# Attention beside a state-space convolution: the skip term goes into the first tap, and the recurrence coefficients are computed per group of chunks

## The chip, the cores and the metric

One core of a Trainium2 chip (trn2) runs the whole program. Its engines are named as in the profile: PE (matmul; PEld are its weight loads), DVE (elementwise work), ACT (activation functions), POOL and SP, which issue transfers. The metric is the device time of one execution in microseconds (us), lower is better.

## The reference

Two independent halves are computed and laid side by side in the output. Half A is a convolution of 2048 steps whose kernel comes from a diagonal complex recurrence; half B is attention with 32 query heads that share one key and one value head.

```python
# A: L = 2048, D = 576 channels, N = 128 states per channel
dt = exp(log_dt)[:, None];  logdA = dt * (A_re + 1j * A_im);  dB = dt * (B_re + 1j * B_im)
P = exp(logdA[:, :, None] * arange(L))                  # powers of the recurrence
K = einsum("dn,dnl,dn->dl", C_re + 1j * C_im, P, dB).real   # one kernel of 2048 taps per channel
y = irfft(rfft(u padded to 2L) * rfft(K padded to 2L))[:L] + u * Dskip
# B: S = 2048, H = 32 heads of 18
q = (x @ wq) by heads;  k = x @ wk;  v = x @ wv
out = softmax(q @ k.T * 18**-0.5) @ v, heads put together, @ wo
```

`u * Dskip` is the skip term. A convolution adds `u[t] * K[0]` to `y[t]`, so `Dskip` can as well be added to `K[0]`, the first tap.

## The kernel before

**Attention.** `main` walks over 1024 tiles of scores (four blocks of 512 queries, 16 pairs of heads, 16 blocks of 128 keys), three tiles to a round. For each tile PE computes the scores `s` (`scores`, L516), ACT takes the exponential into a tile `P` (L527), and PE multiplies by the values into `ops` (L817), a product of four matmuls per two tiles. Query projections `q` (L408) and output projections `op` are work of PE that is put between the rounds. What is left of the last output projection when the last exponential is done is computed in `finish` (`fin`).

**Convolution.** The 576 channels are cut into twelve chunks of 48. `front(k)` makes the kernel of chunk k: `factors` and `tables` (DVE) build tables of powers, `kgen` (PE) multiplies them, and the result goes from `ksb` through DRAM (`kd`) into `kt`, 128 partitions with the first tap in partition 0. `back(k)` convolves: `transform` takes u to its spectrum `us` (matmuls `hu`, `lu`), then `kt` to `ks` (matmuls `hk`, `lk`), DVE multiplies the two (`pt`, `acc`, `sv`, `w`), and the inverse (`iy`) gives the output in `ut`, whose tile is called `u` in the profile. `back(k)` and `front(k + 1)` run beside each other, and both beside the attention. Powers are computed for groups of chunks at once (`BURSTS`: chunk 0, chunks 1 to 4, 5 to 8, 9 to 11), at the group's first chunk.

**What sets the order.** All instructions of PE, DVE and ACT stand in an order that a planner in the kernel makes while the program is built. It keeps its own clocks for PE, DVE and ACT (`Clock`), and the streams of work are Python generators: `yield "p", ready` means that PE work comes next, `yield "v", ready` DVE work; a DVE step is let through when PE's clock has reached `ready` and DVE's clock is at most `ahead` (0.7 to 1.7) past PE's. `lag` compares the convolution's DVE work with `step * RATE`. Engines work through their instructions strictly in this order. All transforms, projections and `kgen` share a single PSUM tile, `f` (`bank`): the next user waits until DVE has copied the previous result out. SP's queue is in program order too.

**Places that the change touches.** `coefficients(k)` (L1046), called for each chunk in `factors` (L1185), computes the products of B, C and dt into `w` by seven DVE instructions on tiles `raw` that `load` (L1012) fetches chunk by chunk. The skip term: `load_u` (L1033) fetches `dsk`, the chunk's `Dskip` broadcast over all partitions, and at the end of `back` DVE computes `ut * dsk` (L1395), to which the results of `iy` are added out of PSUM (L1408):

```python
tt(ut, ut, dsk.unsqueeze(1).broadcast_to([P, 4, NE]), op=ALU.mult)
for hf in range(2):
    ...
    tt(ut[:, sl, :], ut[:, sl, :], ps, op=ALU.add)
```

All DVE instructions that go through the helper `Vector` carry its line in the profile (L119 for two inputs, L123 for copies, L127 for a scalar).

Of the kernel before, what the change touches and what calls it, by code (L numbers as in the profile page):

```python
# [9 lines left out]
F32 = mybir.dt.float32  # L10
# [3 lines left out]
ALU = mybir.AluOpType  # L14
# [3 lines left out]
P = 128  # L18
# [44 lines left out]
ND = 48  # L63
NCK = D // ND
NSB = 2
TB = ND // 4 // NSB
NE = 4 * ND
NF = 28
NB = 11
BURSTS = ((0, 1), (1, 5), (5, 9), (9, 12))  # L70
# [906 lines left out]
class Conv:  # L977
# [31 lines left out]
        pool = lambda n, b: ctx.enter_context(self.tc.tile_pool(name=n, bufs=b))  # L1009
        self.p1 = pool("s_1", 1)  # L1010

    def load(self, k):  # L1012

        if k >= NCK:
            return
        raw = self.p0.tile([P, 4, ND], F32, tag="raw", name=f"raw{k}")
        self.nc.sync.dma_start(raw, self.a["prm"][k])
        self.raw[k] = raw

    def load_burst(self, g):  # L1020

# [11 lines left out]
    def load_u(self, k):  # L1033
        if k >= NCK:
            return
        nc = self.nc
        ut = self.p0.tile([P, 4, NE], F32, tag="u", name=f"u{k}")
        if k < 2:
            nc.vector.memset(ut[0:1, 0, 0:1], 0.0)
        dsk = self.p0.tile([P, NE], F32, tag="dsk", name=f"dsk{k}")  # L1040
        nc.sync.dma_start(ut, self.a["u"][k])
        nc.sync.dma_start(dsk, self.a["dsk"][k].partition_broadcast(P))
        self.ut[k] = ut, dsk
        self.ut_ready[k % 2] = self.k.t + 10.0

    def coefficients(self, k):  # L1046


        V, p1 = self.V, self.pf
        tt = V.tensor_tensor  # L1050
        mu, ad, sb = ALU.mult, ALU.add, ALU.subtract
        raw = self.raw.pop(k)
        w = p1.tile([P, 3, ND], F32, tag="w", name=f"w{k}")
        dt = self.dt[:, (k - self.k0) * ND:(k - self.k0 + 1) * ND]
        tt(raw[:, 0:2, :], raw[:, 0:2, :], dt.unsqueeze(1).broadcast_to([P, 2, ND]), op=mu)
        br, bi, cr, ci = (raw[:, j, :] for j in range(4))
        tt(w[:, 0, :], cr, br, op=mu)
        tt(w[:, 2, :], ci, bi, op=mu)
        tt(w[:, 0, :], w[:, 0, :], w[:, 2, :], op=sb)
        tt(w[:, 1, :], cr, bi, op=mu)  # L1060
        tt(w[:, 2, :], ci, br, op=mu)
        tt(w[:, 1, :], w[:, 1, :], w[:, 2, :], op=ad)
        return w

    def powers(self, g):


        nc, V, p1, K = self.nc, self.V, self.pf, self.k
        tt = V.tensor_tensor
        mu, ad, sb = ALU.mult, ALU.add, ALU.subtract  # L1070
        self.k0, k1 = BURSTS[g]
        nch = k1 - self.k0
        n = nch * ND
        dt, ab = self.next_burst
        self.dt = dt
        shp = [P, n, NB]
        flat = lambda t: t.rearrange("p (n c) -> p n c", c=NB)
        if g == 0:
            both = p1.tile([P, 2, ND * NB], F32, tag="sum", name="pw0")
            r, f = flat(both[:, 0, :]), flat(both[:, 1, :])  # L1080
        else:
            both = p1.tile([P, 2, ND // NSB, 96], F32, tag="tab", name=f"stage{g}").rearrange("p j n c -> p (j n c)")
            r, f = (flat(both[:, j * n * NB:(j + 1) * n * NB]) for j in range(2))
        m = flat(p1.tile([P, 2 * ND * NF], F32, tag="fr", name=f"m{g}")[:, :n * NB])
        ch = lambda t: t.unsqueeze(2).broadcast_to([P, t.shape[1], NB])
        row = lambda j, c: self.pos[:, j, :].unsqueeze(1).broadcast_to([P, c, NB])
        parts = [slice(i * n // (2 if g else 1), (i + 1) * n // (2 if g else 1)) for i in range(2 if g else 1)]
        nc.scalar.activation(dt, dt, AF.Exp)
        yield "v", K.act(0.35) + 0.2, False
        tt(ab, ab, dt.unsqueeze(1).broadcast_to([P, 2, n]), op=mu)  # L1090
        av, bv = ab[:, 0, :], ab[:, 1, :]
        V.tensor_scalar(bv, bv, 1.0 / (2 * math.pi), None, op0=mu)
        yield "v", 0.0, False
        if g > 0:
            for c in parts:
                tt(m[:, c, :], ch(av[:, c]), row(1, c.stop - c.start), op=mu)
                yield "v", 0.0, False
        for c in parts:
            tt(f[:, c, :], ch(bv[:, c]), row(0, c.stop - c.start), op=mu)
            yield "v", 0.0, False  # L1100
        V.tensor_scalar(r, f, MAGIC, -MAGIC, op0=ad, op1=ad)
        yield "v", 0.0, False
        for c in parts:
            tt(f[:, c, :], f[:, c, :], r[:, c, :], op=sb)
            yield "v", 0.0, False
        V.tensor_scalar(r.bitcast(I32), f.bitcast(I32), 0x7FFFFFFF, None, op0=ALU.bitwise_and)
        if g == 0:
            nc.scalar.activation(f, f, AF.Sin, scale=TWO_PI)
            yield "v", 0.0, False
            tt(m, ch(av), row(1, n), op=mu)  # L1110
        else:
            nc.scalar.activation(m, m, AF.Exp)
            K.act(0.1 + 0.833e-3 * n * NB)
        yield "v", 0.0, False
        if g == 0:
            for k in (1, 2):
                self.load(k)
            yield "v", K.v + 0.3, False
        self.burst = g > 0
        yield "b", K.v + 0.3, False  # L1120
        nc.scalar.activation(r, r, AF.Sin, scale=-TWO_PI, bias=self.hp)
        if g > 0:
            nc.scalar.activation(f, f, AF.Sin, scale=TWO_PI)
        else:
            nc.scalar.activation(m, m, AF.Exp)
        yield "v", K.act(3.3 + 1.67e-3 * n * NB) + 0.3, False
        for t in (r, f):
            for c in parts:
                tt(t[:, c, :], t[:, c, :], m[:, c, :], op=mu)
                yield "v", 0.0, False  # L1130
        if nch > 1:
            self.kept = self.dr.tile([P, nch - 1, 2, ND * NB], F32, tag="pw", name=f"pw{g}")
            for j, t in enumerate((r, f)):
                nc.sync.dma_start(self.kept[:, :, j, :], t[:, ND:, :].rearrange("p (k n) c -> p k (n c)", n=ND))
            self.stored = K.t + 9.0
        self.pw = r[:, 0:ND, :], f[:, 0:ND, :]
# [8 lines left out]
    def factors(self, k):  # L1145
# [3 lines left out]
        tt = V.tensor_tensor  # L1149
# [32 lines left out]
        x3 = lambda t: t[:, :, 8:11].unsqueeze(3).broadcast_to([P, ND, 3, 3])  # L1182
        product(x3(pr), x3(pi), r8[:, :, :, 1:4], f8[:, :, :, 1:4], r8[:, :, :, 5:8], f8[:, :, :, 5:8], t1, t2)
        yield "v", 0.0, False
        w = self.coefficients(k)  # L1185
        if k > 0:
            self.load(k + 2)
        if k + 1 == BURSTS[g][1]:
            self.load_burst(g + 1)
        yield "v", 0.0, False  # L1190
# [69 lines left out]
    def front(self, k):  # L1260

        nc = self.nc
        yield from self.factors(k)
        ksb = self.pf.tile([P, 4, NSB, 16, TB], F32, tag="ksb", name=f"ksb{k}")
        yield "v", self.stored, False
        for s in range(NSB):
            yield from self.tables(k, s)
            if s == NSB - 1 and all(k + 1 not in (k0, k1) for k0, k1 in BURSTS):
                self.restore(k + 1)
            yield from self.kgen(k, s, ksb)  # L1270
        while self.kt is not None:
            yield "w", 0.0, False
        kt = self.p1.tile([P, 4, NSB, 16, TB], F32, tag="kt", name=f"kt{k}")
        kd = self.dr.tile([P, 4, NSB * 16 * TB], F32, tag="kd", name=f"kd{k}")
        nc.sync.dma_start(kd, ksb.rearrange("p h s c d -> p h (s c d)"))
        for h in range(4):
            nc.sync.dma_start(kt[32 * h:32 * h + 32].rearrange("p g s c d -> p g (s c d)"), kd[:, h].rearrange("(g p) x -> p g x", p=32))
        self.kt, self.kt_ready = kt, self.k.t + 9.0
# [51 lines left out]
    def back(self, k, kt):  # L1330
# [6 lines left out]
        yield "v", 0.0, False  # L1337
        tt(us[:, 0:4, :], us[:, 4:8, :], us[:, 8:12, :], op=ALU.add)
        ks = p1.tile([P, 12, NE], F32, tag="ks", name=f"ks{k}")
        yield from self.transform(lambda r: kt[:, :, :, 4 * r:4 * r + 4, :].rearrange("p g s b d -> p (g s) (b d)"), ks[:, 4:12, :], f"k{k}", self.kt_ready)  # L1340
        self.kt = None
        k2, kd, ka = ks[:, 0:4, :], ks[:, 4:8, :], ks[:, 8:12, :]
# [48 lines left out]
        tt(w[:, 1:8:6, :], bd[:, 0:2, :], bd[:, 2:4, :], op=ALU.subtract)  # L1391
        tt(w[:, 3:6:2, :], bd[:, 0:2, :], bd[:, 2:4, :], op=ALU.add)
        ready = K.v + 0.3
        yield "v", 0.0, False
        tt(ut, ut, dsk.unsqueeze(1).broadcast_to([P, 4, NE]), op=ALU.mult)  # L1395
        for hf in range(2):
            yield "p", max(ready, K.fill), False
            ps = self.bank(2 * NE, f"iy{k}{hf}").rearrange("p (r n) -> p r n", r=2)
# [6 lines left out]
                if r % 2 == 0:  # L1405
                    yield "p", 0.0, True
            self.evacuate()
            tt(ut[:, sl, :], ut[:, sl, :], ps, op=ALU.add)  # L1408
            self.evacuated()
        nc.sync.dma_start(self.a["outa"][k], ut)  # L1410
        self.load_u(k + 2)
# [83 lines left out]
def layout(inputs):  # L1495

    g = {k: np.asarray(v) for k, v in inputs.items()}
    a = {}
# [30 lines left out]
    a["u"] = np.ascontiguousarray(g["A_u"][0].reshape(4, P, 4, NCK, NSB, 4, TB).transpose(3, 1, 2, 5, 4, 0, 6).reshape(NCK, P, 4, NE))  # L1529
    a["pa"] = np.ascontiguousarray(np.stack([g["A_" + k].T for k in ("A_re", "A_im")], 1))  # L1530
    prm = np.stack([g["A_" + k].T for k in ("B_re", "B_im", "C_re", "C_im")])
    a["prm"] = np.ascontiguousarray(prm.reshape(4, P, NCK, ND).transpose(2, 1, 0, 3))
    a["ldt"] = np.ascontiguousarray(g["A_log_dt"])
    dsk = g["A_Dskip"].reshape(NCK, NSB, 4, 1, TB).transpose(0, 2, 1, 3, 4)
    a["dsk"] = np.ascontiguousarray(np.broadcast_to(dsk, (NCK, 4, NSB, 4, TB)).reshape(NCK, NE))
    i = np.arange(P)[:, None].astype(np.int64)
    f = np.arange(P)[None, :].astype(np.int64)
    th = [2 * np.pi * (((4 * f + 1) * (4 * i + r)) % 2048) / 2048.0 for r in range(4)]
# [30 lines left out]
```

## Time and profile before

| | |
|---|---|
| time, median of 3 runs | 1157.36 us (1155.91 to 1157.46) |
| the profiled execution's own time | 1158.43 us |
| its span in the profile | 1156.7 us |
| granted PE clock, mean | 0.993 |
| PE busy | 1083.0 us (94%) |
| ACT busy | 998.6 us (86%) |
| DVE busy | 995.8 us (86%) |
| moved by DMA | 83.37 MB, mean 72 GB/s |

Times of instructions are in us from the span's start. In the groups of instructions a row reads: line, engine, operation, result and input tiles with shapes, count, then busy time in us, mean ns of one, and idle time of the engine just before them with the instruction that ended it. An fp32 matmul stands in the profile as two records, so x16 in a row of `hk` are eight instructions. Busy time counts overlapping instructions of an engine once.

### The profile page before, as it was taken

How to read it: one execution, taken by the hardware profiler on the slowest of the kernel's cores; microseconds unless marked ns; L12 is line 12 of the kernel's file. 1: busy time of each engine (PE TensorE's matmuls, PEld its weight loads, DVE VectorE, ACT ScalarE, POOL GpSimd, SP SyncE). 2: the span in 40 equal slices, each digit the busy share in tenths (PEclk: the TensorE clock that was granted, in tenths of full speed). 3: DMA queues.
4: the chain of work that ended last, by engine and by line, in shares of the span. 5: the costliest groups of instructions: out<-in, count | busy, mean ns of one | idle time of the engine just before them, and what ended most of it. 6: DMA issues, size and time to landing. Idle time of an engine off the chain costs nothing.

```text
span 1156.7 us, 33067 instructions
## 1 busy us (share of the span) xinstructions
PE 1083.0 (94%) x13886; PEld 393.1 (34%) x13886; DVE 995.8 (86%) x1739; ACT 998.6 (86%) x1052; POOL 141.5 (12%) x257
## 2 busy tenths in 40 slices
PE   6999899999999999899999999989999999999997
PEld 1333333324334333323333333334323333323323
DVE  3788996998998998898899798997898899799683
ACT  3889998888888998998898989887999989899992
POOL 5321322022022000001022000001050000000000
PEclk9999999999999999999999999999999999999999
DMA  7412331114123102112222302102122200311101
GB/s 226 140 46 73 125 119 50 52 42 143 36 74 101 40 28 93 58 40 87 82 85 77 104 21 74 48 29 91 46 84 77 87 30 29 105 48 47 58 29 58
DMA packets 58751, 83.37 MB, mean 72 GB/s; under 512 B 14467, under 2 KB 34679, under 8 KB 58085
## 3 DMA queue, kind: packets, MB, share of 16 engines
q1 hardware_dynamic: 47173, 73.39, 19.2%
q0 software_dynamic: 10848, 7.37, 2.5%
q8 instruction: 111, 1.82, 0.6%
q10 hardware_dynamic: 576, 0.43, 0.2%
q14 instruction: 43, 0.35, 0.1%
HBM read 46.59 MB, written 33.85 MB: 70 GB/s over the span
## 4 chain that ended last, share of the span: by engine, by line
PE 59%; DVE 21%; ACT 12%; issue 6%; DMA 1%; POOL 1%; ACTq 0%; DVEq 0%; POOLq 0%
PE ops L817 24%; PE s L516 15%; ACT P L527 11%; PE op L193 5%; PE q L408 4%; DVE tab L119 4%; PE iy L193 3%; DVE ks L119 3%; PE kg L1253 3%; DVE acc L119 2%; DVE t L119 2%; PE hu L193 1%; PE hk L193 1%; DVE fr L119 1%; PE fin L193 1%
## 5 line engine op out<-in xcount | busy, mean ns | idle before, releaser
L527 ACT ACTIVATE P<-s 128x1024 f32<-128x1024 f32 x992 | 934.6, 1033 | 113.8 <-PE s L516 111.5
L817 PE MATMUL ops<-P,v_sb 128*32 128x512 f32 x4096 | 510.4, 599 | 8.1 <-DVE o L123 7.8
L516 PE MATMUL s<-aug,kaug 55*128 55x512 f16 x2048 | 308.2, 381 | 37.3 <-ACT P L527 33.4
L516 PEld LDWEIGHTS <-kaug 55*128 55x128 f16 x2048 | 91.0, 94 | 372.3 <-issue 326.7
L817 PEld LDWEIGHTS ops<-P,v_sb 128*32 128x32 f32 x4096 | 117.0, 110 | 164.8 <-issue 128.3
L458 POOL DMA_DIRECT2D qd<-qh x116 | 65.6, 572 | 309.6 <-DVE qh L127 307.0
L408 PE MATMUL q<-x,wq_sb 128*32 128x256 f32 x1360 | 83.7, 382 | 0.1
L193 PE MATMUL op<-wo_sb,oT 126*32 126x288 f32 (+1 forms) x1080 | 78.5, 416 | 2.6 <-DVE ob L123 1.4
L119 DVE TENSOR_TENSOR tab<-tab,tt 128x576 f32<-128x576 f32 (+1 forms) x72 | 59.1, 821 | 1.4
L119 DVE TENSOR_TENSOR tab<-tab 128x576 f32<-128x576 f32 (+1 forms) x72 | 58.8, 817 | 0.0
L119 DVE TENSOR_TENSOR tab<-fr,dif 128x576 f32<-128x576 f32 (+1 forms) x72 | 58.8, 817 | 0.0
L119 DVE TENSOR_TENSOR tt<-fr,sum 128x576 f32<-128x576 f32 (+1 forms) x72 | 58.8, 817 | 0.0
L119 DVE TENSOR_TENSOR tab<-sum,fr 128x576 f32<-128x576 f32 (+1 forms) x72 | 58.8, 817 | 0.0
L123 DVE COPY ksb<-kg 128x192 f32<-128x192 f32 x48 | 17.5, 364 | 46.9 <-PE kg L1253 46.6
L408 PEld LDWEIGHTS q<-x,wq_sb 128*32 128x32 f32 x1360 | 39.4, 109 | 38.5 <-issue 13.9
L119 DVE TENSOR_TENSOR acc<-acc,pt 128x1728 f32<-128x1728 f32 (+2 forms) x36 | 48.7, 1352 | 0.1
L119 DVE TENSOR_TENSOR pt<-us,ks 128x1728 f32<-128x1728 f32 (+2 forms) x36 | 48.4, 1351 | 0.1
L1162 POOL MEMSET fr<- 128x192 f32 x24 | 11.9, 580 | 294.0 <-DVE tt L119 192.2
L193 PEld LDWEIGHTS op<-wo_sb,oT 126*32 126x32 f32 (+1 forms) x1080 | 30.6, 110 | 44.2 <-issue 18.3
L525 ACT ACTIVATE P<-s,bias 128x1024 f32<-128x1024 f32 x32 | 32.8, 1123 | 12.9 <-PE s L516 12.7
L1253 PEld LDWEIGHTS kg<-tab 128*32 128x32 f32 x2304 | 35.7, 110 | 22.7 <-DVE ksb L123 7.6
L1253 PE MATMUL kg<-tab 128*32 128x64 f32 x2304 | 41.8, 220 | 1.2 <-DVE tab L119 0.8
(160 smaller groups left out, 1022.4 us busy)
## 6 DMA issues: line engine op xcount, KB each, us to landing
od<-o SPq DMA_DIRECT2D x31, 256.0 KB
aug<-qd SPq DMA_DIRECT2D x124, 55.0 KB
u<-u SPq DMA_DIRECT2D x12, 384.0 KB
kd<-ksb SPq DMA_DIRECT2D x12, 384.0 KB
kt<-kd SPq DMA_DIRECT2D x48, 96.0 KB
outa<-u SPq DMA_DIRECT2D x12, 384.0 KB
pw<-pw SPq DMA_DIRECT2D x8, 528.0 KB
oT<-od SPq DMA_DIRECT2D x16, 252.0 KB
```

The lines of the kernel that those rows point to most:

```text
L119: return self.v.tensor_tensor(out, *a, **k)
L123: return self.v.tensor_copy(out, *a, **k)
L193: nc.tensor.matmul(ps[j:e], w[:, j:e], x, start=start, stop=stop, tile_position=(0, j))
L408: nc.tensor.matmul(ps[o, 256 * f:256 * f + 256], w[:, k, i], xt[:, k, x], start=(k == 0), stop=(k == 4), tile_position=(0, 32 * j))
L458: q.dma_start(qd[h:h + n, row + d:row + d + nd, cs], src[i1:i1 + n * nd, :cs.stop - cs.start])
L516: nc.tensor.matmul(ps[:, j, :], self.kaug[r, kb * P:(kb + 1) * P], t[r, :], start=True, stop=True)
L525: nc.scalar.activation(pt, ps, AF.Exp, bias=self.bias, scale=SCALE / QQ)
L527: nc.scalar.activation(pt, ps, AF.Exp, scale=SCALE / QQ)
L817: nc.tensor.matmul(o_ps[32 * j:32 * j + 32, :], self.v[:, kb, :], pts[2 * n + j // 2][:, j % 2, :], start=(kb == 0), stop=(kb == 15), tile ...
L1162: nc.gpsimd.memset(t[:, :, 0:NF:8], one)
L1253: nc.tensor.matmul(ps[32 * g:32 * g + 32, d, :], t[:, :32], t[:, 32:], start=(j == 0), stop=(j == 1), tile_position=(0, 32 * g))
```

## The change

`Dskip` is no longer multiplied with `u`. `load_u` fetches 48 values into one partition, and `back` adds them to the first tap, `kt[0:1, ..., 0, :]`, before `kt` is transformed; this instruction stands behind a new `yield "v", self.kt_ready`. The results of `iy` are copied, not added, into `ut`. The coefficients of a whole group are computed in `powers(g)`, between the multiplication of the powers and their store, and `factors` takes a slice; `raw` is loaded per group into the buffer of the tiles `sum` (for group 0 of `dif`), once the last tables of the group before are made.

```diff
-    def load(self, k):
-        if k >= NCK:
+    def load(self, g):
+        if g >= len(BURSTS):
             return
-        raw = self.p0.tile([P, 4, ND], F32, tag="raw", name=f"raw{k}")
-        self.nc.sync.dma_start(raw, self.a["prm"][k])
-        self.raw[k] = raw
+        k0, k1 = BURSTS[g]
+        n = (k1 - k0) * ND
+        raw = self.pf.tile([P, 4, n], F32, tag="sum" if g else "dif", name=f"raw{g}")
+        self.nc.sync.dma_start(raw, self.a["prm"][:, :, k0 * ND:k1 * ND])
+        self.raw[g] = raw
...
-        dsk = self.p0.tile([P, NE], F32, tag="dsk", name=f"dsk{k}")
+        dsk = self.p0.tile([1, ND], F32, tag="dsk", name=f"dsk{k}")
         nc.sync.dma_start(ut, self.a["u"][k])
-        nc.sync.dma_start(dsk, self.a["dsk"][k].partition_broadcast(P))
+        nc.sync.dma_start(dsk, self.a["dsk"][k:k + 1, :])
...
-    def coefficients(self, k):
+    def coefficients(self, g, dt):
...
-        w = p1.tile([P, 3, ND], F32, tag="w", name=f"w{k}")
+        n = raw.shape[-1]
+        w = self.pf.tile([P, 3, 4 * ND], F32, tag="w", name=f"w{g}")[:, :, :n]
...
         if g == 0:
-            for k in (1, 2):
-                self.load(k)
             yield "v", K.v + 0.3, False
...
                 tt(t[:, c, :], t[:, c, :], m[:, c, :], op=mu)
                 yield "v", 0.0, False
+        self.coefficients(g, dt)
+        yield "v", 0.0, False
...
-        w = self.coefficients(k)
-        if k > 0:
-            self.load(k + 2)
+        w = self.w[:, :, (k - self.k0) * ND:(k - self.k0 + 1) * ND]
...
-            if s == NSB - 1 and all(k + 1 not in (k0, k1) for k0, k1 in BURSTS):
-                self.restore(k + 1)
+            if s == NSB - 1:
+                if all(k + 1 not in (k0, k1) for k0, k1 in BURSTS):
+                    self.restore(k + 1)
+                else:
+                    self.load(next(j for j, (k0, k1) in enumerate(BURSTS) if k + 1 == k1) + 1)
...
         ks = p1.tile([P, 12, NE], F32, tag="ks", name=f"ks{k}")
+        yield "v", self.kt_ready, False
+        tap = kt[0:1, :, :, 0, :]
+        tt(tap, tap, dsk.rearrange("p (g s d) -> p g s d", g=4, s=NSB), op=ALU.add)
...
-        yield "v", 0.0, False
-        tt(ut, ut, dsk.unsqueeze(1).broadcast_to([P, 4, NE]), op=ALU.mult)
...
-            tt(ut[:, sl, :], ut[:, sl, :], ps, op=ALU.add)
+            V.tensor_copy(ut[:, sl, :], ps)
```

Since the planner counts the DVE work, the whole order shifts somewhat. In chunk 1, on DVE, the spectrum of u (`us1`) and the first copy of the kernel's transform (`sck1` from the PSUM tile `hk10`) stood so before:

```order
L119 TENSOR_TENSOR scu1_2602<-lu11_2744,scu1_2602 128x384 x2
L119 TENSOR_TENSOR us1_2601<-scu1_2602 128x2x192 x4
L119 TENSOR_TENSOR us1_2601<-us1_2601 128x768
L123 COPY sck1_2780<-hk10_2781 128x384
L119 TENSOR_TENSOR fr2_2603<-fr2_2603,w2_2700 128x48x8 x2
```

and now, on DVE in the same place:

```order
L119 TENSOR_TENSOR scu1_2575<-lu11_2716,scu1_2575 128x384 x2
L119 TENSOR_TENSOR us1_2574<-scu1_2575 128x2x192 x4
L119 TENSOR_TENSOR us1_2574<-us1_2574 128x768
L119 TENSOR_TENSOR kt1_2567<-kt1_2567,dsk1_350 1x8x6
L123 COPY sck1_2773<-hk10_2774 128x384
L119 TENSOR_TENSOR sum2_2707<-fr2_2576 128x1344
```

The addition to the tap, `kt1<-kt1,dsk1`, stands behind the whole spectrum of u, and the copy of `hk10` directly behind it. The matmuls `hk10` read `kt1` and so come after it. On PE, from the last matmuls of u's transform (`lu11`) to `hk10`, before:

```order
L193 MATMUL lu11_2744<-u1_352,dft_sb_98 32x192 x8
L817 MATMUL ops0_5_2720<-P0_10_1_2676,v_sb_115 32x512 x2
...
L516 MATMUL s0_10_4_2763<-aug0_110,kaug_109 128x512
...
L516 MATMUL s0_10_5_2769<-aug0_110,kaug_109 128x512
L193 MATMUL hk10_2781<-kt1_2594,dft_sb_98 32x192 x8
```

and now:

```order
L193 MATMUL lu11_2716<-u1_348,dft_sb_98 32x192 x4
L817 MATMUL ops0_5_2742<-P0_10_0_2651,v_sb_115 32x512 x2
...
L516 MATMUL s0_10_4_2751<-aug0_110,kaug_109 128x512
...
L516 MATMUL s0_10_5_2757<-aug0_110,kaug_109 128x512
L817 MATMUL ops0_5_2742<-P0_10_1_2687,v_sb_115 32x512 x2
...
L193 MATMUL hk10_2774<-kt1_2567,dft_sb_98 32x192 x8
```

One more product (`ops`, four matmuls) stands ahead of `hk10` than before. At the end of PE's program, behind the last product, the rest of the output projection (`fin`, with `oT` as input) was before:

```order
L193 MATMUL fin0_14385<-wo_sb_107,oT3_13148 32x288 x16
L193 MATMUL fin1_14386<-wo_sb_107,oT3_13148 32x288 x8
L666 MATMUL bc_14384<-rc_last_14383,b4_14078 128x256
...
L193 MATMUL fin2_14387<-wo_sb_107,oT3_13148 32x288 x16
...
L193 MATMUL fin3_1_14474<-wo_sb_107,oT3_13148 32x288 x12
```

and is now:

```order
L193 MATMUL fin0_14329<-wo_sb_107,oT3_13053 32x288 x8
L193 MATMUL fin1_14330<-wo_sb_107,oT3_13053 32x288 x12
L666 MATMUL bc_14328<-rc_last_14327,b4_14013 128x256
L193 MATMUL fin2_14331<-wo_sb_107,oT3_13053 32x288 x16
...
L193 MATMUL fin3_1_14406<-wo_sb_107,oT3_13053 32x288 x8
```

With the rows left out, 68 such matmuls stood there and 52 stand there now: the convolution's last chunk is done earlier in the order, and 16 matmuls more of the output projection stand among the last rounds.

More of the change, by code (lines that the diff above doesn't have):

```diff
@@ L1039, in load_u @@
             nc.vector.memset(ut[0:1, 0, 0:1], 0.0)
-        dsk = self.p0.tile([P, NE], F32, tag="dsk", name=f"dsk{k}")
+        dsk = self.p0.tile([1, ND], F32, tag="dsk", name=f"dsk{k}")
         nc.sync.dma_start(ut, self.a["u"][k])
-        nc.sync.dma_start(dsk, self.a["dsk"][k].partition_broadcast(P))
+        nc.sync.dma_start(dsk, self.a["dsk"][k:k + 1, :])
         self.ut[k] = ut, dsk
         self.ut_ready[k % 2] = self.k.t + 10.0
-    def coefficients(self, k):
-        V, p1 = self.V, self.pf
-        tt = V.tensor_tensor
+    def coefficients(self, g, dt):
+        tt = self.V.tensor_tensor
         mu, ad, sb = ALU.mult, ALU.add, ALU.subtract
-        raw = self.raw.pop(k)
-        w = p1.tile([P, 3, ND], F32, tag="w", name=f"w{k}")
-        dt = self.dt[:, (k - self.k0) * ND:(k - self.k0 + 1) * ND]
-        tt(raw[:, 0:2, :], raw[:, 0:2, :], dt.unsqueeze(1).broadcast_to([P, 2, ND]), op=mu)
+        raw = self.raw.pop(g)
+        n = raw.shape[-1]
+        w = self.pf.tile([P, 3, 4 * ND], F32, tag="w", name=f"w{g}")[:, :, :n]
+        tt(raw[:, 0:2, :], raw[:, 0:2, :], dt.unsqueeze(1).broadcast_to([P, 2, n]), op=mu)
         br, bi, cr, ci = (raw[:, j, :] for j in range(4))
@@ L1062, in coefficients @@
         tt(w[:, 1, :], w[:, 1, :], w[:, 2, :], op=ad)
-        return w
+        self.w = w
     def powers(self, g):
@@ L1074, in powers @@
         dt, ab = self.next_burst
-        self.dt = dt
         shp = [P, n, NB]
@@ L1531, in layout @@
     prm = np.stack([g["A_" + k].T for k in ("B_re", "B_im", "C_re", "C_im")])
-    a["prm"] = np.ascontiguousarray(prm.reshape(4, P, NCK, ND).transpose(2, 1, 0, 3))
+    a["prm"] = np.ascontiguousarray(prm.transpose(1, 0, 2))
     a["ldt"] = np.ascontiguousarray(g["A_log_dt"])
-    dsk = g["A_Dskip"].reshape(NCK, NSB, 4, 1, TB).transpose(0, 2, 1, 3, 4)
-    a["dsk"] = np.ascontiguousarray(np.broadcast_to(dsk, (NCK, 4, NSB, 4, TB)).reshape(NCK, NE))
+    a["dsk"] = np.ascontiguousarray(g["A_Dskip"].reshape(NCK, NSB, 4, TB).transpose(0, 2, 1, 3).reshape(NCK, ND))
     i = np.arange(P)[:, None].astype(np.int64)
```

## The prediction, made before the changed kernel ran

> **What bounds the kernel now.** I read the page's first part and its chain first.
>
> ```profile
> span 1156.7 us, 33067 instructions
> PE 1083.0 (94%) x13886; PEld 393.1 (34%) x13886; DVE 995.8 (86%) x1739; ACT 998.6 (86%) x1052; POOL 141.5 (12%) x257
> PE 59%; DVE 21%; ACT 12%; issue 6%; DMA 1%; POOL 1%; ACTq 0%; DVEq 0%; POOLq 0%
> ```
>
> Three engines are nearly full, and the chain of work that ended last runs over PE for 59% of the span and over DVE for 21%. So neither engine's busy time can be booked in full: of a microsecond taken from DVE I expect about 0.21 us back, of a microsecond in which PE stands about 0.59 us lost, unless a place shows more. Where there is little else to do, the rhythm is that of PE and ACT, as the chain shows near the end:
>
> ```profile
> 1110.28 1.94 ACT P L527 x2
> 1116.35 1.94 ACT P L527 x2
> ```
>
> Six exponentials in 6.07 us. The change touches neither them nor any matmul. It works on DVE, so I looked next at who waits for DVE, and for whom DVE waits:
>
> ```profile
> PEld ops L817 <- DVE o L123: 14.9, 20, 3.5
> PEld lu L193 <- DVE scu L123: 9.6, 15, 1.0
> PEld lk L193 <- DVE sck L123: 6.7, 10, 1.2
> DVE u L119 <- PE iy L193: 14.5, 12, 2.5
> DVE sck L123 <- PE hk L193: 7.5, 10, 1.4
> ```
>
> PE waits some tens of microseconds in all for copies out of PSUM, and DVE waits as much for matmuls of the convolution. No row has `hk` waiting for a transfer. The two engines hand work to each other, and the change adds one more such hand-over per chunk.
>
> **The change part by part.** *Work taken from DVE.* The rows of the groups that go, and those that price what comes:
>
> ```profile
> L119 DVE TENSOR_TENSOR u<-u,dsk 128x768 f32<-128x768 f32 x12 | 11.4, 949 | 0.0
> L119 DVE TENSOR_TENSOR u<-u,iy 128x384 f32<-128x384 f32 x24 | 13.3, 553 | 15.0 <-PE iy L193 14.5
> L123 DVE COPY scu<-hu 128x384 f32<-128x384 f32 x24 | 13.3, 555 | 13.8 <-PE hu L193 13.7
> L119 DVE TENSOR_TENSOR w<-raw 128x48 f32<-128x48 f32 x48 | 7.8, 205 | 0.4
> L119 DVE TENSOR_TENSOR w<-w 128x48 f32<-128x48 f32 x24 | 5.0, 208 | 0.8
> L119 DVE TENSOR_TENSOR raw<-raw,dt 128x96 f32<-128x96 f32 x12 | 3.0, 249 | 0.0
> L119 DVE TENSOR_TENSOR t<-pw 128x192 f32<-128x192 f32 x36 | 11.2, 355 | 0.3
> L119 DVE TENSOR_TENSOR t<-fr,w 128x384 f32<-128x384 f32 x24 | 12.2, 548 | 0.3
> ```
>
> The twelve multiplications by `dsk` are 11.4 us. Twelve additions of 48 values come for them; the nearest row has the same length on 128 partitions, 205 ns, so 2.5 us: 8.9 us less. The copy of `iy` in place of the addition gains nothing: the copy `scu<-hu` of equal size out of PSUM takes 555 ns, the addition 553.
>
> The coefficients take 7.8 + 5.0 + 3.0 = 15.8 us. Per group, by busy time: group 0 as now, 0.25 + 4 x 0.163 + 2 x 0.208 = 1.3 us. Groups 1 and 2 (192 wide): one instruction of 384 at 0.51, four of 192 at 0.31, two that follow their source at 0.355, 2.46 us each. Group 3 (144 wide), by straight lines between these, 2.1 us. Together 8.3 us, so 7.5 us less, with 56 instructions fewer. The Trainium skill (VectorE: DVE Perf Modes, the section on the errata of SBUF sources) gives a fixed 58 cycles per instruction at 0.96 GHz, by which 56 fewer would save an estimated 3.4 us. The rows price a 48-wide instruction at 163 ns against 311 for four times the width, which is the larger saving, and I go by them.
>
> So DVE loses 8.9 + 7.5 = 16.4 us of 995.8. What that is worth is bounded by nothing on the one side. On the other stand the places where the chain itself runs over the instructions that go:
>
> ```profile
> 136.95 0.95 DVE u L119
> ...
> 156.19 0.18 DVE raw L119
> 156.39 0.34 DVE w L119 x2
> 156.75 0.46 DVE w L119 x3
> 157.24 0.22 DVE w L119
> ...
> 929.30 0.18 DVE raw L119
> ```
>
> There are three such runs of `raw` and `w` on the chain (at 156, 380 and 929 us, 1.2 us each) and the one full `u` of 0.95 us with two remnants of 0.53 us, 5.1 us in all.
>
> *The new wait.* The addition to the tap stands on DVE behind `us<-us`, the last step of u's spectrum, and `hk` must now wait for it. Before, `hk` needed `kt` and a free PSUM tile, no more. In the time-ordered view, chunks 0, 1 and 11:
>
> ```profile
> 101.02 0.13 PEld L193 LDWEIGHTS hk<-kt,dft_sb 128*32 128x32 f32 x4 [0.30 <-issue]
> 102.39 0.95 DVE L119 TENSOR_TENSOR us<-us 128x768 f32<-128x768 f32 x1
> ...
> 216.77 0.48 PEld L193 LDWEIGHTS hk<-kt,dft_sb 128*32 128x32 f32 x16 [0.23 <-issue]
> 216.78 0.86 PE L193 MATMUL hk<-kt,dft_sb 128*32 128x192 f32 x16
> 217.66 0.96 DVE L119 TENSOR_TENSOR us<-us 128x768 f32<-128x768 f32 x1
> 218.54 0.55 DVE L123 COPY sck<-hk 128x384 f32<-128x384 f32 x1
> ...
> 1087.37 0.95 DVE L119 TENSOR_TENSOR us<-us 128x768 f32<-128x768 f32 x1
> 1087.90 0.48 PEld L193 LDWEIGHTS hk<-kt,dft_sb 128*32 128x32 f32 x16 [0.35 <-issue]
> ...
> 103.72 1.26 DVE L127 TENSOR_SCALAR stage<-stage 128x2112 f32<-128x2112 f32 x1
> ```
>
> `hk` starts before `us<-us` has ended: by 2.32, 1.85 and 0.42 us here. Over chunks 0 to 11 the lead is 2.32, 1.85, 1.33, 0.85, 1.89, 0.17, 1.15, -4.30, 1.24, 2.49, -4.81 and 0.42 us: ten of twelve positive, 13.7 us in sum. With 0.2 us for each of the ten additions PE would stand 15.7 us if nothing in the order moved. That is the upper bound; the lower one is nothing. The order takes part of it away: a product, 0.86 us of PE, more stands ahead of `hk` in chunk 1, two in chunks 2 and 11, and in chunks 4 and 8 projections, whose PSUM tile has to be copied out first anyway, stand there now. In chunk 0 the scalar instruction over 2112 elements of the last row here now comes between `us<-us` and the tap, 1.26 us. Left over are 3.8, 1.2, 1.1, 0.4, 1.4 and 2.7 us in chunks 0, 1, 3, 5, 6 and 9, 10.4 us. I take these, nearer to the upper end because the order is known; at PE's share of 59% they cost 6.1 us.
>
> Behind the tap on DVE stands, in seven chunks (0, 1, 2, 5, 6, 9 and 11), the copy of `hk`, which now has to wait for the whole matmul block of 0.86 us. Before, DVE was still busy with `us<-us` meanwhile. So DVE loses 6.0 of the 16.4 us again, and 10.4 are left, at 21% a gain of 2.2 us. What else is queued behind the tap is the front's work and the copy of `ops`, for which PE waits at the start of each head group.
>
> The tap does not wait for its transfer: the last `kt` went out here, 5.7 us ahead of the place where the tap will stand.
>
> ```profile
> 1080.65 1.96 SPq L1277 DMA_DIRECT2D kt<-kd  x4
> 1136.26 2.91 PE fin L193 x48
> ...
> 1.21 0.70 SPq L1030 DMA_DIRECT2D ab<-pa  x1
> 1.95 0.58 SPq L1017 DMA_DIRECT2D raw<-prm  x1
> ```
>
> *The end.* Four blocks of the output projection move from `fin` into the last rounds. A row of `fin` has 6 blocks in 2.91 us, 0.485 each, so the tail is 1.9 us shorter. If the last rounds have no room on PE, they lengthen by as much. I take 1.0 us of gain, between 0 and 1.9.
>
> *Transfers.* On SP eight loads of `raw` go (twelve before, four now), and the broadcasts of `dsk` become single rows; they hid behind everything before, and the gain is nothing. The load of a group's `raw` waits in SP's queue for the tables of the chunk before, at the place where the other chunks have `restore` with the same wait. The first `raw` is now fetched in four pieces per partition, like `ab` in two: 0.70 us of issue against 0.58, ahead of x, for which PE's first matmul waits. I book 0.2 us, between 0 and 0.7.
>
> *Sum.* -2.2 + 6.1 - 1.0 + 0.2 = +3.1 us on the profiled execution's 1158.43 us (its span of 1156.7 and 1.7 around it), that is 1161.5. This execution lies 1.1 us above the median of the runs; on the median of 1157.36 the forecast is 1160.5 us.
>
> **The rivals.** *DVE's time counts, the wait does not: faster.* Behind `hk` PE soon waits for DVE anyway (`lk` for `sck` 6.7 us, `ops` for `o` 14.9 us), so a wait at the tap may only take the place of one a few instructions later, while PE and DVE run in step from there. Then the 5.1 us that stand on the chain come back whole and the tail its 1.9: 7.0 us less, 1150.4 us. The chain's shares between 112 and 137 us and between 1000 and 1050 us:
>
> ```profile
> by line: DVE acc L119 23.7%; DVE ks L119 21.1%; DVE pt L119 15.6%; issue 13.6%; DVE sv L119 7.9%; DVE u L119 5.2%; DVE sck L119 4.1%; DVE w L119 3.3%; DVE sh L127 2.3%; DVE qh L127 1.7%; DVE ql L131 1.7%; DVE ab L135 1.3%; DVE aw L127 1.2%;
> by line: PE ops L817 35.2%; PE s L516 21.2%; PE op L193 15.6%; ACT P L527 15.3%; issue 4.6%; PE lk L193 2.9%; PE hk L193 2.9%; PE lu L193 1.6%; DVE o L123 1.4%; ACTq L527 0.1%
> ```
>
> For this rival speaks that the first stretch runs on DVE almost alone; against it, that the second has hardly any DVE on it, while the taps stay there too. It decides when the waits of `hk` for the tap, summed, stay under about 3 us beyond what other waits there shrink.
>
> *No change.* The rounds of PE and ACT set the time, and both the work taken away and the wait disappear in the 14% of the span in which DVE and ACT are idle: 1157.4 us.
>
> *The wait counts in full: much slower.* DVE lags further behind the planner's clock than the order allows for, and each `hk` stands its whole lead: 15.7 - 2.2 - 1.0 + 0.2 = +12.7, 1170.1 us. The longer blocks of coefficients at the heads of groups 1 to 3 work in the same direction: 1.1, 1.1 and 0.8 us more in one piece, 3.0 us, where powers are awaited. The Trainium skill (Perfetto Trace Analysis, Optimizing Scalar/DVE Operations) states the rule behind this: where DVE is not saturated but causes bubbles on other engines, breaking instructions up lets work be done sooner; the change does the opposite. No row here shows a long block being waited for by itself.
>
> That the change does not do what it says is excluded: the order has twelve additions on one partition and no multiplication by `dsk` left.
>
> **How the numbers follow.** I give the forecast (about +0.5 to +6 us) 0.42, the faster rival 0.30, no change 0.12, the full wait 0.16. A difference within 0.2% (2.3 us) is about what a measurement of this kernel can't tell from no change; of the forecast's share 0.08 lies within it. So faster 0.30, same 0.20, slower 0.50. The likeliest case gives 1160.5 us, by its own terms 1157 to 1164. The range takes in most of the faster rival and half of the full wait: 1149 to 1168 us.
>
> **What would show it.** In the profile of the changed kernel: `kt<-kt,dsk` twelve times at about 0.2 us; a row of PEld `hk` waiting for DVE `kt`, about 10 us in ten or fewer waits; DVE `sck` waiting for `hk` longer than 7.5 us; DVE busy near 979 us; the last `fin` some 2 us shorter. I am wrong if `hk` hardly waits for `kt`, or if it does and PE's waits for `o`, `scu` and `sck` shrink by more.

## The result and the profile after

The changed kernel takes 1160.92 us (median of 19 runs, 1157.15 to 1165.57); the kernel before, run beside it, 1157.13 (1153.08 to 1160.39). The ratio is 1.0035 (95% interval 1.0026 to 1.0045): 3.8 us slower, where 3.1 were forecast. The sum came out, but not by its terms. One execution among all of these runs, of run 12 (1373.47 us at a granted PE clock of 0.751), is left out of its ratio.

First the page of the changed kernel, its first part and its chain:

```profile
span 1157.9 us, 33019 instructions
PE 1079.9 (93%) x13886; PEld 392.0 (34%) x13886; DVE 982.1 (85%) x1687; ACT 999.0 (86%) x1052; POOL 141.1 (12%) x257
PE 60%; DVE 19%; ACT 12%; issue 6%; DMA 2%; POOL 1%; ACTq 0%; DVEq 0%; POOLq 0%
```

DVE works 13.7 us less (995.8 before), PE 3.1 us less, ACT as long as before, and the span is 1.2 us longer. (This execution lies 1.3 us below the median of its kernel's runs, that of before 1.3 us above; so the traces show 1.2 of the 3.8 us.) The new groups on DVE, with their columns busy us and mean ns:

```profile
L119 DVE TENSOR_TENSOR kt<-kt,dsk 1x48 f32<-1x48 f32 x12 | 2.3, 190 | 0.0
L123 DVE COPY u<-iy 128x384 f32<-128x384 f32 x24 | 13.3, 553 | 12.4 <-PE iy L193 12.4
L119 DVE TENSOR_TENSOR w<-raw 128x192 f32<-128x192 f32 x8 | 2.5, 353 | 0.1
L119 DVE TENSOR_TENSOR w<-raw 128x48 f32<-128x48 f32 x4 | 0.7, 204 | 0.0
```

The tap, the copy and the coefficients (nine groups, two of them shown, 8.5 us in all) cost what the prediction gave them. Now the waits (total us, times, longest), those that answer to the rows of before:

```profile
PEld ops L817 <- DVE o L123: 19.3, 21, 2.2
PEld lk L193 <- DVE sck L123: 10.4, 14, 1.1
PEld lu L193 <- DVE scu L123: 9.3, 14, 0.7
DVE u L123 <- PE iy L193: 12.4, 12, 3.4
DVE sck L123 <- PE hk L193: 7.1, 11, 1.9
```

No row has `hk` waiting for the tap, where 10.4 us in up to ten waits were forecast. (The view of the tile `kt` has one wait of `hk`, 1.3 us in chunk 8, but a matmul `lk`, which reads `kt` too, ended it; the kernel before has two of that kind, 2.8 us.) `sck` did not wait longer for `hk` (7.1 against 7.5), either. What grew on PE are `lk`'s waits for `sck` (10.4 against 6.7) and those of `ops` for `o` (19.3 against 14.9). More than these grew what DVE waits for projections. Of before, then of the changed kernel (`qh` is made from `q`, `part` holds the partial sums of the last output projection):

```profile
DVE qh L127 <- PE q L408: 5.9, 3, 2.9
L119 DVE TENSOR_TENSOR part<-part,op 128x288 f32<-128x288 f32 x7 | 3.1, 447 | 4.1 <-PE op L193 4.1
```

```profile
DVE qh L127 <- PE q L408: 21.9, 5, 7.2
L119 DVE TENSOR_TENSOR part<-part,op 128x288 f32<-128x288 f32 x11 | 5.0, 452 | 13.5 <-PE op L193 13.5
```

Together these waits are 25.4 us longer, more than the DVE work that went; the prediction has no term for them. The timeline in chunk 1 shows why `hk` is free:

```profile
219.03 0.13 PEld L193 LDWEIGHTS hk<-kt,dft_sb 128*32 128x32 f32 x4 [0.30 <-issue]
219.61 0.96 DVE L119 TENSOR_TENSOR us<-us 128x768 f32<-128x768 f32 x1
220.48 0.19 DVE L119 TENSOR_TENSOR kt<-kt,dsk 1x48 f32<-1x48 f32 x1
220.60 0.54 DVE L123 COPY sck<-hk 128x384 f32<-128x384 f32 x1
221.83 0.16 PEld L193 LDWEIGHTS lk<-kt,dft_sb 128*32 128x32 f32 x8 [0.42 <-issue]
```

`hk` starts 1.45 us ahead of the tap. `transform` takes its halves in the order `for half in (1, 0)`, and half 1 reads `src(2)` and `src(3)`, the blocks 8 to 15 of `kt`. The tap writes block 0, which only half 0, `lk`, reads. `lk` comes behind the copy `sck<-hk` anyway, and that copy stands behind the tap on DVE. In six of the seven chunks in which `hk` would have been held (0, 1, 2, 5, 6, 9 and 11) it begins before the tap does, and in chunk 11 in the middle of it. So the wait on which the forecast rested does not exist, and 3.8 us remain to be explained.

### The profile page after: what moved, and what is told of

The parts are those of the page before. It is cut to its first block, busy times and chain, and to the rows that moved or that the text cites. A ratio compares the mean times of both kernels' runs of the same rounds, so it can differ in the third digit from the quotient of the medians.

```text
span 1157.9 us, 33019 instructions
## 1 busy us (share of the span) xinstructions
PE 1079.9 (93%) x13886; PEld 392.0 (34%) x13886; DVE 982.1 (85%) x1687; ACT 999.0 (86%) x1052; POOL 141.1 (12%) x257
## 3 DMA queue, kind: packets, MB, share of 16 engines
q8 instruction: 111, 1.82, 0.6%
## 4 chain that ended last, share of the span: by engine, by line
PE 60%; DVE 19%; ACT 12%; issue 6%; DMA 2%; POOL 1%; ACTq 0%; DVEq 0%; POOLq 0%
PE ops L817 25%; PE s L516 16%; ACT P L527 11%; DVE tab L119 4%; PE op L193 4%; PE q L408 4%; DVE ks L119 3%; PE iy L193 3%; PE kg L1251 3%; DVE acc L119 2%; DVE pt L119 1%; PE hu L193 1%; PE lk L193 1%; PE hk L193 1%; DVE tt L119 1%
```

## The experiments

The planner writes the engines' order from a cost that each DVE instruction is charged with. A change of DVE work is therefore two changes: of the work and of the order. The first experiments separate them. (The numbers are labels; there is no run 9. The diffs show the lines that matter and leave out the rest.)

**The order held, the work changed, and the reverse.** A stand-in charges the planner without issuing an instruction (`Ghost` is a name and a shape):

```diff
 # run 1: all of the change, charged as before
-        self.coefficients(g, dt)
-        yield "v", 0.0, False
+        self.coefficients(g, dt)            # issued, not charged
+        # in factors(): charge seven steps of 48 per chunk
-        yield "v", self.kt_ready, False
-        tt(tap, tap, dsk...)
+        nc.vector.tensor_tensor(tap, tap, dsk...)
         ready = K.v + 0.3
+        yield "v", 0.0, False
+        K.dve(ut, 1.04e-3, ut)              # the multiplication that is gone
 # run 2: the work of before, charged as in the changed kernel
+        yield "v", self.kt_ready, False
+        K.dve(Ghost("kt", 1, ND), 1.04e-3, Ghost("kt"))
-        yield "v", 0.0, False
-        tt(ut, ut, dsk...)
+        nc.vector.tensor_tensor(ut, ut, dsk...)
```

> All of the change's instructions (tap, copies of iy, coefficients per group, the new transfers), but the planner is charged as before, so TensorE's instructions stand word for word in the order of before. Theory A, the reshuffled order costs the time and the shorter work saves some: faster than before by 2 to 5 us, about 0.997, 1152 to 1155 us against 1157. Theory B, the new instructions themselves cost it (the tap, the long coefficient blocks, the four raw loads): as slow as the changed kernel, 1.0035, about 1161 us. Theory C, the work is worth nothing and costs nothing here: 1.000.

> The instructions of before (u*dsk, additions of iy, coefficients per chunk, no tap), but the planner is charged as in the changed kernel, so TensorE's instructions stand word for word in the changed kernel's order. Theory A: slower than the changed kernel by what the work saves, 1163 to 1166 us, about 1.006. Theory B: as before, 1157 us, 1.000. Theory C: 1161 us, 1.0035.

Measured against the kernel before, with TensorE's order identical in each column:

| | order of before | order of the changed kernel |
|---|---|---|
| work of before | 1 | 1.0188 (1.0171 to 1.0205), 1177.12 us |
| the change's work | 0.9995 (0.9985 to 1.0005), 1156.38 us | 1.0035 (1.0026 to 1.0045), 1160.92 us |

In the old order the change's instructions cost nothing: theory B, under which tap, coefficient blocks or loads cost the time, falls. They save hardly anything either, as theory C has it for this run. Run 1's busy times:

```profile
PE 1080.0 (94%) x13886; PEld 391.4 (34%) x13886; DVE 980.9 (85%) x1683; ACT 998.5 (87%) x1052; POOL 139.5 (12%) x257
```

14.9 us less on DVE than before give 0.6 us. The new order costs 0.40%, 4.6 us, and that is the whole loss. Its instructions are the same but for four additions `part<-part,op`, 2.0 us of DVE: the four blocks of the output projection that moved from `fin` into the rounds are added up there. The longer waits for projections come with the order, too: those of `qh` and `part` are 6.7 and 4.1 us in run 1, 19.5 and 13.5 in run 2. Theory A has the sign of the loss, but none of the three had the last corner. DVE work that the planner doesn't know of cost more than its length in this order: 15.2 us more on DVE (997.3 against 982.1), 1.53% or 17.7 us more. On run 2's page (busy times, chain), and in its waits:

```profile
PE 1081.3 (92%) x13886; PEld 391.7 (33%) x13886; DVE 997.3 (85%) x1743; ACT 999.3 (85%) x1052; POOL 141.1 (12%) x257
PE 49%; DVE 35%; ACT 8%; issue 6%; DMA 2%; SPq 1%; DVEq 0%; ACTq 0%
ACT P L533 <- PE s L522: 129.8, 194, 3.0
```

DVE's share of the chain goes from 19 to 35%. The last row is the drum of this kernel: 1,024 exponentials of the same length, so what an order loses ahead of the last one shows in what ACT waits for scores. The same row of before, the changed kernel, run 1 and run 11 (1153.0 us, below):

```profile
ACT P L527 <- PE s L516: 111.5, 185, 3.1
ACT P L527 <- PE s L516: 114.2, 189, 3.0
ACT P L533 <- PE s L522: 109.1, 185, 3.1
ACT P L533 <- PE s L522: 103.6, 186, 3.3
```

In these five the kernel is the slower the longer this wait is.

**The two halves of the change, each re-planned.** Run 3 takes the change without its skip term (the lines of `dsk`, tap and `iy` as before), run 4 without the coefficients:

```diff
 # run 3, against the changed kernel
+        tt(ut, ut, dsk...)
-        tt(tap, tap, dsk...)
-            V.tensor_copy(ut[:, sl, :], ps)
+            tt(ut[:, sl, :], ut[:, sl, :], ps, op=ALU.add)
 # run 4, against the changed kernel
+        w = self.coefficients(k)
-        self.coefficients(g, dt)
```

> Only the coefficients per group, with the planner re-planning freely: a third order. DVE busy about 987 (7 less). Theory A: anywhere between 1152 and 1164 us, and not adding up with the other half of the change to +3.8. Theory B, if the long blocks at the group heads are the cause: about 1160 us; if the tap is: 1156.

> Only the skip term in the first tap, re-planned freely: a fourth order. DVE busy about 988 (8 less). Theory A: anywhere between 1152 and 1164 us, with no relation to the other half. Theory B, if the tap is the cause: about 1160 us; if the coefficient blocks are: 1155.

Run 3: 1152.43 us, 0.9961 (0.9948 to 0.9974). Run 4: 1163.37 us, 1.0057 (1.0043 to 1.0071). Both take work away from DVE (987.5 and 989.7 us), one is 4.5 us faster and one 6.6 slower. Taken alone the two would fit the tap as the cause; but runs 1 and 11 issue the tap in other orders and lose nothing. Their sum, +2.1 us, is not far from +3.8, but it is a sum of two orders, as the later runs show.

**The gate before the tap.** The change brings a new point at which the planner waits for the transfer of `kt`:

```diff
-        yield "v", self.kt_ready, False
         tap = kt[0:1, :, :, 0, :]
```

> The changed kernel without the point before the tap at which the planner waits for the transfer of kt; the tap follows the last step of u's spectrum at once. Theory gate (this point lets VectorE's convolution work stand and so spoils the order): back to 1157 us or less, ratio up to 1.000. Theory scatter (any new order lies somewhere, whatever made it): between 1152 and 1164 us, and the places of loss are elsewhere than with the gate.

1161.26 us, 1.0031 (1.0017 to 1.0044), as the changed kernel, in yet another order: the loss is there without the gate.

**The wait that was forecast, made real.**

```diff
         tt(tap, tap, dsk...)
+        hk_tap = kt[0:1, :, :, 8, :]
+        nc.vector.tensor_scalar(hk_tap, hk_tap, 0.0, None, op0=ALU.add)
```

> The changed kernel, its order word for word on TensorE, with one more instruction on one partition behind each tap, 48 values, that adds zero to what hk reads: now hk does have to wait for the tap, as the prediction said of the change itself. By the starts in the changed kernel's trace hk would stand 0.95, 1.64, 1.21, 0.55, 0.81, 0.45 and 0.05 us in chunks 0, 1, 2, 5, 6, 9 and 11, 5.7 us in all and 0.2 more for each of those seven, 7.1 us. Theory of the prediction, at TensorE's 59%: 4.2 us more than the changed kernel, about 1165 us, 1.007; whole: 1168. Theory that the wait takes the place of later ones (lk for sck, ops for o): 1160 to 1162 us.

1166.43 us, 1.0075 (1.0062 to 1.0089), 0.40% or 4.6 us above the changed kernel in the same order. The timeline in chunk 1, and what `sck` waited in the whole run:

```profile
221.50 0.17 DVE L1345 TENSOR_SCALAR kt<-kt 1x48 f32<-1x48 f32 x1
221.75 0.51 PEld L193 LDWEIGHTS hk<-kt,dft_sb 128*32 128x32 f32 x16 [2.11 <-issue]
221.78 0.86 PE L193 MATMUL hk<-kt,dft_sb 128*32 128x192 f32 x16 [1.23 <-issue]
```

```profile
DVE sck L123 <- PE hk L193: 11.6, 13, 1.9
```

In each of the seven chunks `hk` now starts within 0.1 us of the added instruction's end, and PE's matmuls stood 1.07, 1.23, 0.80, 0.67, 0.94, 0.52 and 0.00 us before it, 5.2 us in all (7.1 expected). The profile puts most of this down to "issue", so its rows by releaser (1.2 us of PE `hk` for `kt`) show only part of the wait. `sck` does wait longer for `hk`, 11.6 us against 7.1, as the prediction's second step said. So the mechanism exists and, with the added work, the total is near the price given to it (4.2 expected here); it is only not in this change. The twelve added instructions are 2.1 us of DVE work that the planner doesn't know of. At run 2's price that would be an estimated 2.4 us, which leaves 2.2 for the wait; this run doesn't separate the two.

**The planner's pace.** The convolution may take `RATE` us of DVE work per step of the attention, set to the work of before. Run 7 scales it to the smaller work; run 8 makes the mismatch in the kernel before; run 10 goes the other way in the changed kernel.

```diff
-RATE = 1.84
+RATE = 1.82     # run 7, the changed kernel; 1.86 in run 8 (before) and run 10 (changed)
```

> The changed kernel with the planner's pace of the convolution RATE 1.82 in place of 1.84, in the proportion of the work that it counts (920.4 against 930.0 us). Theory pace (with less work counted the same pace runs the convolution ahead of the attention): the loss goes, 1157 us or less. Theory scatter: another order, anywhere between 1152 and 1166 us. No sensitivity: 1161 us.

> The kernel before, not an instruction changed, with RATE 1.86: the mismatch of pace and work that the change brings, without the change. Theory pace: slower by 3 to 5 us, 1160 to 1162 us. Theory scatter: a new order that lies anywhere within some 6 us on either side. No sensitivity: 1157 us, 1.000.

> The changed kernel with RATE 1.86, the opposite of the run with 1.82, which ended its convolution too late and lost 26 us at the end. If the changed kernel's loss comes from a convolution that lags the attention: faster than 1161 us, 1150 to 1158. If any new order just lies somewhere: between 1152 and 1166 us. If a higher pace is what costs, as in the kernel before with 1.86: about 1166 us.

Run 7: 1187.64 us, 1.0269 (1.0253 to 1.0286). Run 8: 1161.82 us, 1.0040 (1.0024 to 1.0055). Run 10: 1157.93 us, 0.9997 (0.9983 to 1.0012). The theory of pace falls with run 7, which none of the expectations covers. The reason stands in its trace; the chain behind its last exponential, which begins at 1140.31, and the busy times from there (length, then PE, PEld, DVE, ACT, POOL and the granted clock), of run 7 and of before:

```profile
1143.30 2.56 DVE acc L119
1155.74 1.96 DVE sv L119 x4
1161.78 2.79 PE iy L193 x32
1164.57 2.93 PE fin L193 x40
```

```profile
1140.31:1183.40 43.09, 20.37 (x260) 9.51 (x252) 28.52 (x38) 1.79 (x3) 0.00 (x0) 0.75 0.11 39
```

```profile
1134.02:1156.70 22.68, 16.26 (x228) 7.49 (x220) 8.92 (x16) 1.79 (x3) 0.00 (x0) 0.94 0.16 56
```

At 1.82 the last chunk isn't done when the exponentials are: products, `sv`, `iy` and only then `fin` follow alone, 43.1 us against 22.7. TensorE, half idle there, was granted 0.75 of its clock, against 0.94. (The Trainium skill, TensorE: Matmul & The Clock Gate, part 1, says that the throttled state is the default and activity releases it; these two rows agree with it.) Run 10 lies where the theory of a lag put it, but where scatter put it, too. Against a lag speaks that the last matmul `iy` starts at 1120.1 us in the changed kernel, earlier than before (1128.9). Run 8 is the point: not an instruction changed, a constant of the planner by 1%, and the kernel before is 4.6 us slower, as much as the whole change makes. (Its granted clock was lower as well, 0.9918 in the mean against 0.9941 of before beside it. At the 0.8 us per thousandth of the last section that is an estimated 1.8 of the 4.6 us; whether the order lowers the clock isn't shown.) The same 1% makes the changed kernel 4.4 us faster (run 10).

**The same instructions in three more orders.** In these runs every instruction of the change is issued, and only what the planner is told of the skip term differs:

```diff
+        known = False       # run 11; k < 6 in run 12, k >= 6 in run 13
+        if known:
             yield "v", self.kt_ready, False
+            K.dve(tap, 1.04e-3, tap)
-        tt(tap, tap, dsk...)
+        nc.vector.tensor_tensor(tap, tap, dsk...)
+        if not known:       # charge the multiplication that is gone
+            yield "v", 0.0, False
+            K.dve(ut, 1.04e-3, ut)
```

> All of the change's instructions, but the planner is told of the coefficients per group only; for the skip term it goes on charging the multiplication and the additions that are gone. TensorE's order is word for word that of the run with the coefficients alone (1152.4 us). Theory order: 1150 to 1152.5 us, 0.994 to 0.996: the whole change is then faster than the kernel before by 5 us, and the +3.8 us are the order's alone. Theory that tap and skip term cost time themselves: 1156 us or more.

> The same instructions, the planner told of the skip term's new cost in chunks 0 to 5 only. If the loss of the changed kernel against the run before this one is made where the traces show it, behind exponential 544 (chunks 6 to 8): 1150 to 1155 us. If it is made early: about 1160 us. If an order can't be split so: anywhere between 1150 and 1165.

> The same instructions, the planner told of the skip term's new cost in chunks 6 to 11 only; up to chunk 5 the order is that of the coefficients alone. If the loss is made behind exponential 544: 1157 to 1162 us. If it is made early: 1150 to 1154 us. If an order can't be split so: anywhere between 1150 and 1165, and not the complement of the run with chunks 0 to 5.

Run 11: 1153.04 us, 0.9957 (0.9937 to 0.9976). Run 12: 1160.05 us, 1.0034 (1.0015 to 1.0053). Run 13: 1163.34 us, 1.0046 (1.0027 to 1.0065). The whole change in run 3's order is 0.43% faster than the kernel before; it and run 3 are the fastest of all that were run. Telling the planner the truth for the first half of the chunks costs 0.77% against that, for the second half 0.89%, for all of them 0.78%. That does not add up, so the loss has no one place: each of these is an order of its own. Run 13's size is uncertain: its mean granted clock was 0.9896, run 11's 0.9943, by which an estimated 3.8 us of the difference would go with the clock. What is left, about 0.56%, doesn't add up either.

What a worse order looks like can be read where run 11 and the changed kernel differ most, from exponential 544 to 704. The windows of the changed kernel, of run 11 and of before (bounds, length, and busy PE, PEld, DVE, ACT, POOL):

```profile
619.56:799.10 179.54, 169.44 (x2346) 64.65 (x2342) 168.20 (x283) 151.58 (x162) 10.87 (x21) 1.00 0.18 58
```

```profile
620.95:789.73 168.78, 166.38 (x2242) 61.79 (x2246) 156.45 (x264) 151.14 (x161) 7.83 (x15) 1.00 0.18 57
```

```profile
621.82:796.36 174.54, 167.62 (x2214) 62.03 (x2210) 158.73 (x272) 150.88 (x162) 7.25 (x14) 1.00 0.18 58
```

The same 160 exponentials take 179.5, 168.8 and 174.5 us. In the changed kernel the planner put 168.2 us of DVE work beside them, in run 11 156.5. DVE is busy for 94 and 93% of the stretch, and between these two 11.8 us more work go with 10.8 us more time; PE and ACT wait, where DVE's queue holds back a copy. That the work alone sets the length is not shown: in the order of before, run 1 has 3.9 us less DVE work here (154.9 against 158.7) and is 0.5 us shorter (174.0 against 174.5). The waits in these windows, of the changed kernel and of run 11:

```profile
ACT P L527 <- PE s L516: 27.5, 40, 3.0
PEld ops L817 <- DVE o L123: 5.6, 4, 2.2
PE ops L817 <- DVE o L123: 4.2, 4, 1.5
```

```profile
ACT P L533 <- PE s L522: 17.8, 37, 1.5
PEld ops L823 <- DVE o L129: 0.5, 1, 0.5
```

ACT waits 9.7 us longer for scores, nearly all of the 10.8 us. Part is given back at the end: work that is done early is no longer left there. From the start of the last exponential to the end run 11 needs 26.5 us, the changed kernel 20.6, the kernel before 22.6. The same 160 exponentials in runs 12 and 13:

```profile
620.22:800.40 180.18, 169.63 (x2322) 63.72 (x2318) 163.93 (x276) 151.15 (x161) 9.20 (x18) 1.00 0.18 56
```

```profile
618.74:788.08 169.34, 167.27 (x2266) 62.69 (x2270) 157.16 (x267) 151.15 (x161) 7.83 (x15) 1.00 0.18 57
```

So this stretch's loss comes with what the planner is told in chunks 0 to 5, although the taps of chunks 6 and 7 stand in it (667 and 742 us in the changed kernel); run 13 is free of it here and loses elsewhere, 6.4 us against run 11 in the next 96 exponentials (109.6 against 103.2).

## Why the prediction was right, and by what error

Direction and size came out (3.8 against 3.1 us), by a step that is false and one that was missing. That they came out is luck: 6.1 us were booked for a wait that isn't there, and 4.6 us of an order that was not priced took its place. By the prediction's own sign ("if `hk` hardly waits for `kt`") its account is wrong.

- *"`hk` must now wait for it"*: false. The dependency was taken from the tile, `kt`, and not from the slices: the tap writes block 0, `hk` reads blocks 8 to 15. Measured: no wait of `hk` for the tap, against 10.4 us; its +6.1 us were not there. Nor did DVE lose the 6.0 us behind the tap: `sck` waited 7.1 us for `hk`, against 7.5 before. The code alone would have told it. With the dependency made real PE stands 5.2 us, and the cost is at most 4.6 us in this order.
- *DVE loses 16.4 us*: 14.9 in the same order (run 1), 13.7 in the trace after. By the rows of the groups it is 16.4; in the sum over the engine, where overlapping instructions count once, less goes, and the new order adds the four additions of `part`. The coefficients take 8.5 us now (8.3 forecast), the tap 2.3 (2.5), the copy 553 ns (555). The rule of the Trainium skill weighed there (VectorE: DVE Perf Modes, 58 cycles fixed, an estimated saving of 3.4 us) falls short: 15.8 - 8.5 is 7.3 us, and between the 48- and the 192-wide row, 204 and 353 ns, lie 1.03 ns per element, which leaves 154 ns per instruction that do not depend on its length. The same section of the page says itself that its row under-predicts, with about 150 cycles measured as the fixed term; by that an estimated 156 ns, with which these rows agree.
- *Such a microsecond is worth DVE's share of the chain, 21%*: mis-sized. In an order that stays it was worth 4% (0.6 of 14.9 us, at most 1.7 by the interval), so the -2.2 us were -0.6. Run 11 against run 3, again in one order, has 8.5 us less on DVE and stands at 0.9957 against 0.9961. Time added to DVE behind the planner's back cost 116% (run 2). The share prices neither.
- *The order*: the missing term. The prediction read from the new order how many products stood ahead of each `hk`, but took everything else in it as worth what it was before. The re-planned order costs 4.6 us.
- *The end, -1.0 us*: 2.0 us (22.6 to 20.6); `fin` has 168 records for 200, the four blocks of eight records that were forecast, but their work stands in the rounds, so it is a part of the order's account.
- *The faster rival* took the time to fall by the 5.1 us of the chain and the tail's 1.9, 1150.4 us. Run 11 comes near it with 1153.0, but run 1, with the chain's places unchanged, shows that it isn't those 5.1 us that do it. *No change* is what the work alone gives (run 1). *The full wait's* second reason, long coefficient blocks, costs nothing that run 1 or run 3 show; the rule on breaking instructions up (the Trainium skill, Perfetto Trace Analysis, Optimizing Scalar/DVE Operations) finds no case here.

What stays open is which single decisions of the planner make one order better than another. The windows show that the changed kernel loses where more DVE work stands beside the exponentials than they leave room for, not what steers the planner into that. One difference that was not tried by itself is how many blocks of the output projection stand in the rounds: the additions `part<-part,op` are 3 in runs 3 and 11, 7 before and in run 1, 11 in the changed kernel. It can't be the whole of it, since runs 12 and 13 have 7 and are slow, and run 10 has 12 and is as fast as before.

## What to carry to other kernels

Where a planner writes the order from costs, an edit of the work is also a throw of the order: hold the order by charging the old costs and measure the work, then hold the work and measure the order. Here the work was worth 0.6 us and the order 4.6, and a 1% change of one constant moved both kernels about as far; so a saving of this size is worth looking for several orders, and keeping the best. And before a wait is booked, compare the slices that are written and read, not the names of the tiles.

## What the runs showed of the hardware

What DVE work costs is not what its absence gains: some 15 us of it were worth 0.6 us when taken out of the order of before and 17.7 us when put into that of the changed kernel. (These are two orders, so how much lies in the direction and how much in the order isn't separated; 8.5 us taken out of run 3's order gave nothing that can be measured, either.) And the granted TensorE clock scatters from execution to execution: over the 19 runs of the changed kernel it lay between 0.988 (1165.57 us) and 0.998 (1157.15), 8.4 us, about 0.8 us for each thousandth. The order's whole effect is half of that scatter, so it shows only in the median of many executions.
